# Attention rows of two units merged in DRAM, down weights loaded once a block, last block in two halves: a transformer pair of layers on one core

## The chip, the cores and the metric

One core of one Trainium2 chip. The metric is the device time of one execution in microseconds (us), taken over several executions; the profile is of one such execution, and its span is 2 to 3 us shorter than the time. Engines: PE (matmul; PEld is its weight loads), ACT (scalar engine: exponentials and GELU), DVE (vector engine), POOL, and SP, whose queue (SPq in the listings) issues nearly all the DMAs.

## The reference

Two layers with shared weights, S = 2048 tokens, D = 512, 32 heads of 16, F = 1792:

```python
x = x + A(layernorm(x), wqkv, wo)          # softmax attention, 32 heads of 16
x = x + B(layernorm(x), w_gate, w_up, w_down)  # (gelu(x@w_gate) * (x@w_up)) @ w_down
# ... the same two lines once more
```

## The kernel before

The kernel writes its program with a small list scheduler of its own: a model of each engine's time decides, while the program is built, in which fixed order the instructions stand. A "unit" is four heads of one block of 512 query rows; a layer has 4 blocks of 8 units, and a unit has 64 score tiles of 128 keys by 512 queries. Most tiles get their exponential on ACT, in instructions of two or three tiles. Some go to DVE, by an integer trick with one evacuation and three shifts ("vector tiles"). The feed-forward of a finished block ("post") is fed in pieces into the gaps of the next block's attention.

The parts that the change touches (cuts are marked `# ...`):

```python
NWR = 6                                   # slots for gate, up and down weight chunks, 256 KB each
OS = sb("fOS", [128, HB + 4, 512], F32)   # unnormalised attention rows, one slot a unit
RB = sb("fRB", [128, 2, 512], F32)        # broadcast reciprocals
ATS = sb("fATS", [128, 2, 512], F16)      # odd units' rows before they move to their partitions
# ...
for layer in range(n_rep):                # the list of weight loads, in order of use
    for qb in range(NQB):
        tail = layer == n_rep - 1 and qb == NQB - 1
        wlist += [("g", i) ...] + [("u", i) ...]
        wlist += [("d", i) for _ in range(1 if tail else 2 if qb == NQB - 1 and NQB > 1 else 4) for i in range(NFT // 2)]
# ...
def normalise(layer, qb, gs, half):       # for a group of units (four; 4, 2, 1, 1 at the very end)
    # ... check and reciprocal of the gathered denominators on DVE, stored to DRAM
    def spread():
        # per unit: four DMAs broadcast the reciprocals to RB, POOL multiplies OS by RB;
        # an even unit's product goes to AT, an odd unit's to ATS and by four DMAs to AT
        for j in range(4):
            move(0, "rb%d_%d" % (slot, j), RB[32 * j:32 * j + 16, slot, :], AP(RSC, ...), ...)
# ...
def post(layer, qb):
    # wait for the rows of all 8 units; output projection, layernorm,
    # 7 chunks of gate, GELU, 7 of up, then down for each token tile (weights loaded again)
# ...
def keep_clock():   # dummy matmuls, put in while PE would idle (meant to keep its clock up; no run here tests that)
    # four matmuls of 17x512, on zeros
```

A DMA is a job for SP: it is put into the queue in the order in which the model sees its inputs ready, and SP issues strictly in that order.

## Time and profile before

Median 1682.3 us (1681.39 to 1684.56, 3 runs).

| | before |
|---|---|
| span | 1680.1 us |
| end of the last attention product | 1610.4 us |
| tail after it | 69.7 us |
| ACT busy before that point / waits on scores | 1552.0 / 45.5 us |
| dummy matmuls, about 55 ns each | 2396 |

Lines of the page of the kernel before: busy time and share of each engine; ACT's busy tenths in 40 slices; the chain of waits by engine; and two groups of instructions (count, busy us, mean ns, then the idle time before them and its main cause).

```profile
PE 1574.3 (94%) x15555; PEld 490.9 (29%) x15614; DVE 1378.3 (82%) x2329; ACT 1561.3 (93%) x1348; POOL 208.6 (12%) x222
...
ACT  7899999999999999999899999999999999999932
...
ACT 53%; PE 34%; DVE 10%; POOL 1%; DMA 1%; issue 1%; SPq 0%; DVEq 0%; POOLq 0%
...
L1344 PE MATMUL fPS<-fONB,fZV 128*17 128x512 f16 x2396 | 186.5, 385 | 2.3 <-POOL fQMASK L362 1.5
...
L788 POOL TENSOR_TENSOR fAT<-fOS,fRB 128x512 f16<-128x512 f32 x32 | 43.1, 1345 | 815.6 <-DMA fRB<-rscr 815.6
```

PE's 94% is not work alone: the dummies (L1344) are in it, and their timeline (276 in 15.07 us) gives 131 us for all 2396. Apart from that, the Trainium skill ("Trainium Kernel Development and Optimization", section "Performance Expectations") calls matmul busy time a bad metric for the distance to the peak, because matmuls are pipelined. This trace agrees: a dummy's record is 385 ns long, and the dummies start 55 ns apart. POOL's 815.6 us of waiting costs nothing, as POOL is 12% busy and makes up 1% of the chain.

The waits of ACT (line, and what ended the wait: total us, times, longest):

```profile
ACT fPT L1204 <- PE fPS L1191: 45.5, 74, 5.3
ACT L919 <- PE fPS L592: 30.3, 1, 30.3
```

The windows view, cut at the end of the last attention product (each busy time in us, instructions in brackets):

```profile
core 0: us, PE busy (x) PEld busy (x) DVE busy (x) ACT busy (x) POOL busy (x), PEclk, DMA share, GB/s
0.00:1610.43 1610.43, 1510.60 (x14945) 461.85 (x15001) 1354.28 (x2282) 1551.98 (x1333) 205.85 (x218) 1.00 0.23 66
1610.43:1680.10 69.67, 63.73 (x611) 29.06 (x613) 24.03 (x47) 9.32 (x15) 2.78 (x4) 0.98 0.26 73
```

So ACT's time up to the last product is 1552.0 us busy and 58.4 idle, of which 45.5 are waits for scores.

The timeline of the tail of the kernel before (start us, length us, engine, line, operation, count; in brackets the idle time before it):

```profile
1610.47 0.69 DVE L829 COPY fOS<-fPS 128x512 f32<-128x512 f32 x1 [1.46 <-PE fPS L1324]
...
1611.21 15.07 PE L1344 MATMUL fPS<-fONB,fZV 128*17 128x512 f16 x276 [0.78 <-DVE fOS L829]
...
1615.99 1.69 SPq L277 DMA_DIRECT2D fRB<-rscr  x4
1619.20 1.28 POOL L788 TENSOR_TENSOR fATS<-fOS,fRB 128x512 f16<-128x512 f32 x1 [17.34 <-DMA fRB<-rscr]
1620.51 3.12 SPq L277 DMA_DIRECT2D fAT<-fATS  x4
...
1626.45 3.40 PE L592 MATMUL fPS<-fWO,fAT 128*128 128x512 bf16 x15 [0.16 <-issue]
...
1638.77 24.35 PE L592 MATMUL fPS<-fXNT,fWR 128*128 128x512 f16 x112
...
1663.17 12.03 PE L953 MATMUL fPS<-fWR,fHT 128*128 128x512 bf16 x54
...
1675.96 2.25 SPq L277 DMA_DIRECT2D out_dram<-fXNT  x4
```

Copy-out, normalisation behind four DMA hops while PE runs 276 dummies, projection at 1626.4, layernorm, 112 gate and up matmuls, down, stores. Elsewhere the two longest waits of ACT are 5.3 us near the start and this one at the layer boundary (timeline of the kernel before):

```profile
820.35 2.37 ACT L1204 ACTIVATE fPT<-fPS 128x1024 bf16<-128x1024 f32 x2 [4.79 <-PE fPS L1191]
```

### The profile page before, as it was taken

The numbers are of one execution on the slowest core, as the hardware profiler recorded it, in microseconds if no ns is written. First come the engines' busy times: TensorE is split into PE (matmuls) and PEld (weight loads), VectorE is DVE, ScalarE is ACT, GpSimd is POOL, SyncE is SP. The second block draws the span as 40 slices with busy tenths as digits, with TensorE's granted clock in tenths as the row PEclk, the third lists the DMA queues.
The fourth block names the chain that finished last, engine by engine and source line by source line (L and its number), as shares of the span: only waits on it lengthen the run. The fifth ranks groups of instructions, "written<-read, shape, count | busy, mean of one in ns | idle before, by whom it ended". The sixth has DMA issues, their size and how long they took to land.

```text
span 1680.1 us, 36981 instructions
## 1 busy us (share of the span) xinstructions
PE 1574.3 (94%) x15555; PEld 490.9 (29%) x15614; DVE 1378.3 (82%) x2329; ACT 1561.3 (93%) x1348; POOL 208.6 (12%) x222
## 2 busy tenths in 40 slices
PE   9999999999899989999999999999999999999998
PEld 3332222222222223233332322222222222222233
DVE  7899998879998799977643899988899878897853
ACT  7899999999999999999899999999999999999932
POOL 3222010101201021000600211101011100101010
PEclk9999999999999999999999999999999999999999
DMA  4100001252014410125224000024301251014303
GB/s 139 52 2 18 2 19 33 67 176 59 17 45 123 135 42 9 44 63 171 74 58 138 27 19 17 22 58 132 113 18 39 68 168 56 17 45 145 107 16 109
DMA packets 140285, 111.82 MB, mean 67 GB/s; under 512 B 13904, under 2 KB 129872, under 8 KB 140112
## 3 DMA queue, kind: packets, MB, share of 16 engines
q1 hardware_dynamic: 136416, 104.78, 21.5%
q0 software_dynamic: 2112, 4.19, 0.9%
q8 instruction: 127, 2.08, 0.5%
q10 hardware_dynamic: 1584, 0.39, 0.1%
q14 instruction: 46, 0.38, 0.1%
HBM read 97.78 MB, written 6.82 MB: 62 GB/s over the span
## 4 chain that ended last, share of the span: by engine, by line
ACT 53%; PE 34%; DVE 10%; POOL 1%; DMA 1%; issue 1%; SPq 0%; DVEq 0%; POOLq 0%
ACT fPT L1204 50%; PE fPS L592 10%; PE fPS L1324 9%; PE fPS L1191 8%; DVE fPP L1277 4%; PE fPS L953 3%; DVE fPI L1241 3%; PE fPS L1344 2%; ACT fHT L1157 2%; POOL fVD L669 1%; DVE fHT L916 1%; DVE fHT L939 1%; ACT L1157 1%; PE fPS L656 1%; DVE fQ L636 0%
## 5 line engine op out<-in xcount | busy, mean ns | idle before, releaser
L1204 ACT ACTIVATE fPT<-fPS 128x1536 bf16<-128x1536 f32 (+1 forms) x1302 | 1487.6, 1286 | 49.1 <-PE fPS L1191 45.5
L1241 DVE TENSOR_SCALAR fPI<-fPS 128x512 int16<-128x512 f32 x843 | 570.5, 684 | 94.0 <-PE fPS L1191 88.1
L1191 PE MATMUL fPS<-fQ,fKT 32*128 32x512 f16 x4096 | 513.6, 385 | 50.4 <-ACT fPT L1204 36.2
L1324 PE MATMUL fPS<-fPT,fVP 128*17 128x512 bf16 x3253 | 469.5, 383 | 11.7 <-DVE fOS L829 5.4
L1277 DVE TENSOR_SCALAR fPP<-fPI 128x2048 int16<-128x2048 int16 (+3 forms) x723 | 445.5, 646 | 8.1 <-PE fPS L1324 2.4
L1324 PE MATMUL fPS<-fPP,fVD 128*17 128x512 f16 x2529 | 410.0, 382 | 10.6 <-DVE fPP L1277 5.7
L1191 PEld LDWEIGHTS fPS<-fQ,fKT 32*128 32x128 f16 x4096 | 128.8, 91 | 535.3 <-ACT fPT L1204 383.8
L1324 PE MATMUL fPS<-fPI,fVP 128*17 128x512 f16 x843 | 255.1, 382 | 1.6 <-DVE fPP L1277 0.9
L592 PE MATMUL fPS<-fXNT,fWR 128*128 128x512 f16 x896 | 221.7, 381 | 10.9 <-DVE fHT L939 6.0
L1344 PE MATMUL fPS<-fONB,fZV 128*17 128x512 f16 x2396 | 186.5, 385 | 2.3 <-POOL fQMASK L362 1.5
L1324 PEld LDWEIGHTS fPS<-fPT,fVP 128*17 128x17 f16 x3253 | 108.8, 88 | 164.0 <-issue 92.6
L788 POOL TENSOR_TENSOR fAT<-fOS,fRB 128x512 f16<-128x512 f32 x32 | 43.1, 1345 | 815.6 <-DMA fRB<-rscr 815.6
L1324 PEld LDWEIGHTS fPS<-fPP,fVD 128*17 128x17 f16 x2529 | 99.3, 88 | 120.3 <-issue 47.4
L939 DVE TENSOR_TENSOR fHT<-fPS,fHT 128x512 bf16<-128x512 f32 x112 | 76.4, 688 | 57.6 <-PE fPS L592 41.2
L953 PE MATMUL fPS<-fWR,fHT 128*128 128x512 bf16 x402 | 113.7, 382 | 7.6 <-issue 5.7
L592 PEld LDWEIGHTS fPS<-fXNT,fWR 128*128 128x128 bf16 x896 | 72.8, 98 | 128.9 <-DVE fHT L939 19.6
L916 DVE CAST fHT<-fPS 128x512 bf16<-128x512 f32 x98 | 66.6, 686 | 25.7 <-PE fPS L592 25.3
L1344 PEld LDWEIGHTS fPS<-fONB,fZV 128*17 128x17 f16 x2396 | 56.3, 91 | 64.4 <-issue 30.6
L1324 PEld LDWEIGHTS fPS<-fPI,fVP 128*17 128x17 f16 x843 | 58.3, 88 | 37.5 <-issue 14.2
L669 POOL TENSOR_SCALAR fVD<-fVP 128x544 f16<-128x544 f16 (+1 forms) x48 | 54.7, 1142 | 96.4 <-DVE fVP L677 93.8
L548 POOL TENSOR_SCALAR fLNS<-fMV 128x4 f32<-128x4 f32 (+1 forms) x17 | 5.2, 306 | 430.5 <-DVE fMV L541 430.4
L788 POOL TENSOR_TENSOR fATS<-fOS,fRB 128x512 f16<-128x512 f32 x32 | 42.4, 1325 | 78.2 <-DMA fRB<-rscr 78.2
(60 smaller groups left out, 700.3 us busy)
## 6 DMA issues: line engine op xcount, KB each, us to landing
fWR<-in_B_w_down_dram SPq DMA_DIRECT2D x189, 256.0 KB, 3.0
fWR<-in_B_w_gate_dram SPq DMA_DIRECT2D x56, 256.0 KB, 3.1
fWR<-in_B_w_up_dram SPq DMA_DIRECT2D x56, 256.0 KB, 2.9
fRB<-rscr SPq DMA_DIRECT2D x256, 32.0 KB, 1.9
fX<-in_A_x_dram POOLq DMA_DIRECT2D x4, 1024.0 KB, 5.6
xscr<-fX SPq DMA_DIRECT2D x16, 256.0 KB, 2.5
fX<-xscr SPq DMA_DIRECT2D x4, 1024.0 KB, 5.6
fAT<-fATS SPq DMA_DIRECT2D x128, 16.0 KB, 1.8
```

Of the source, the lines that this page charges most:

```text
L592: ins = e.matmul(bank(bs[0])[:, 0:cols], lhsT=l, rhs=r_, start=(i == 0), stop=(i == n - 1))
L669: job("pool", 2, [(lambda e, dst=dst, src=src, ph=ph: e.tensor_scalar(dst, src, 2.0 ** (-ph / NPH), None, op0=ALU.mult), [("VP", c, k) for ...
L788: job("pool", 1, [(lambda e: e.tensor_tensor(dst, OS[:, os_, :], RB[:, slot, :], op=ALU.mult), [("OS", os_)] + [("RB", slot, j) for j in r ...
L916: evac_job(1, b, [(lambda e: e.tensor_copy(HT[:, ft, :], bank(b)), [BK[b]], [("HT", ft)], 0.6)], got(("gate", layer, qb, ft)))
L939: (lambda e: e.tensor_tensor(HT[:, ft, :], bank(b), HT[:, ft, :], op=ALU.mult), [BK[b], ("HT", ft)], [("HT", ft)], 0.62)], got(("up", laye ...
L953: ins = e.matmul(bank(b)[:, 0:D], lhsT=HT[:, ft, i * 128:(i + 1) * 128], rhs=WR[:, s, jj * D:(jj + 1) * D], start=(ft == 0), stop=(ft == N ...
L1191: ins = e.matmul(bank(b), lhsT=KT[32 * j:32 * j + 32, (u % NG) // 2, kt * 128:(kt + 1) * 128], rhs=Q[32 * j:32 * j + 32, (layer * NU + u) ...
L1204: o = sch.op("act", lambda e: e.activation(PT[:, p, 0:512 * na].rearrange("p (a b) -> p a b", a=na), PS[:, b0:b0 + na, :], ACTF.Exp, scale ...
L1241: dve(0, [(lambda e: e.tensor_scalar(PI[:, gi, 512 * r:512 * (r + 1)], bank(bd), DBIAS, 0.0, op0=ALU.add, op1=ALU.max), [BK[bd]], [("PI", ...
L1277: shifts.append((s, [(lambda e: e.tensor_scalar(PP[:, s, 0:512 * n], PI[:, gi, 0:512 * n], int(OCT) * ph // NPH, None, op0=ALU.add), [("PI ...
L1324: ins = e.matmul(PS[32 * j:32 * j + VW, ACC, :], lhsT=l, rhs=r_, start=a, stop=z, tile_position=(0, 32 * j), skip_group_check=True)
L1344: ins = e.matmul(PS[32 * j:32 * j + VW, ACC, :], lhsT=ZV[:, :], rhs=ones, start=False, stop=False, tile_position=(0, 32 * j), skip_group_c ...
```

## The change

The intent, as far as the code shows it: (1) rows of each unit are put out to DRAM at once; a pair of units then comes back as one full 128-partition tile, with one broadcast and one POOL product, so the odd rows need no second move. (2) That frees SBUF for a seventh weight slot, and down weights stay in seven slots for all token tiles of a block. (3) The last block's attention runs as two halves of 256 query rows, so that half of its feed-forward runs under the second half's attention; score tiles there are pairs of 256 columns. With them come smaller edits: keys and values of the second head group earlier at the start, pieces paced by cost with a tolerance for the first eight, and layernorm scales for two tiles at a time.

```diff
-    NWR = 6
+    NWR = 7
-    NOS = HB + 4
+    NOS = NPART + 1
-    NRB = 2
+    NRB = 1
-    ATS = sb("fATS", [128, 2, 512], F16)
+    OP = sb("fOP", [128, NRB, 512], F32)
+    OSD = nc.dram_tensor("oscr", (NOD // 2, 128, 512), F32, kind="Internal")
 # ... weight list: down once, the last block twice; six spare slots in WK, WV, WQ at the very end
+            halves = layer == n_rep - 1 and qb == NQB - 1 and NQB > 1
+            for h in ((0, 1) if halves else (None,)):
+                wlist += [("g", i) ...] + [("u", i) ...]
+                wlist += [("d", i) for i in range(NFT // 2)]
 # ... normalise: a pair comes back from DRAM, one product
+            move(0, "op%d" % slot, OP[:, slot, 0:qn], OSD[ds[0] // 2, :, 0:qn], ...)
+            move(0, "rb%d" % slot, RB[:, slot, 0:qn],
+                 AP(RSC, (half * NG + i) // 2 * 8 * 512, [[512, 8], [0, 16], [1, qn]]), ...)
+            # one POOL product into AT[:, c, q0:q0 + qn]
 # ... evac: each unit's rows go out by four DMAs; groups of 6 and 2 units
+            sizes = [NG - 2, 2] if NG > 2 else [NG]
+                    move(0, "os%d_%d" % (s, j), OSD[d // 2, 32 * j + 16 * (d % 2):..., 0:qn], OS[...], ...)
 # ... segments of the last block
+            for h in range(2):
+                segs += [(layer, NU - NG + g, HALF[h], 0, 2 * NKT) for g in order(layer, NQB - 1, h)]
 # ... start, pacing, layernorm
-                    kv(up, b, layer == 0)
+                    kv(up, b, layer == 0 and (up > 1 or b > PRE))
-                        pace["n"] += 1
+                        if first <= 8:
+                            p.tol = 1.0
+                        pace["n"] += (p.cost + 0.1) / 0.71
+        def scale(lo):      # layernorm scale and apply for two tiles
+            hi = min(lo + 2, nt)
 # ...
```

## The prediction

> **What bounds it now.** Busy table: PE 94%, ACT 93%, DVE 82%, POOL 12%; DMA 67 GB/s. Half of the chain of waits is the exponential on ACT. PE is not truly full: 2396 of its matmuls are clock-keeping dummies, about 55 ns each (276 in 15.07 us), some 131 us. ACT sets the pace until the last attention product at 1610.5 us; its score waits sum to 45.5 us, the longest near the start (5.3) and the layer boundary. Then a serial tail of 69.6 us, ACT nearly idle: copy-out and normalisation until 1626.4 (276 dummies), projection and layernorm until 1638.8, 112 gate/up matmuls 24.3, down 12.0, last adds and stores 4.9.
>
> **What changes.**
> 1. Merged rows: 64 POOL products (1.27 us) become 28 plus 8 half-wide, about 41 us for 85; 256 broadcast and 128 odd-row DMAs go, 288 put-outs, 36 loads and 36 broadcasts come. POOL is off the chain: about 0.
> 2. Down weights: 189 loads become 65, 32 MB less. The only weight landing on the chain was 4.9 us, with ACT still 98% busy. Worth 0 to 2 us.
> 3. Halves: half a feed-forward runs under the last attention. From the instruction order after the last attention product: 26 and 28 down of 512 columns and 8 projection (0.2165 us each), 112 gate/up of 256 columns (estimate 0.108, half of that), 444 dummies (0.0546). Sum 50 us, plus 0.5 copy-out and 4 at the end: a tail of 55 for 69.6. Gate/up saves 12, projection and layernorm 4, last adds 1. Down hardly shrinks: the first half's down spills past the attention. The wait before the projection stays: its broadcast is queued behind the first half's stores and weight loads, and 256 dummies precede it.
> 4. Cost: vector tiles 843 to 829, so 14 more on ACT (0.427 us by issue spacing) 6 us; two table loads 2.6; half a block's GELU 3.1: 12 us more ACT in the attention. PE: 14 us more real work.
> 5. Gains there: earlier keys and values at the start, gentler pacing, two-tile layernorms. Dummies before the tail fall from 1984 to 1692, 16 us of PE, most at the start and the layer boundary. I expect 10 to 16 of ACT's 45 us of score waits to go.
>
> **256 columns.** The Trainium skill, "TensorE: Matmul & The Clock Gate", gives a sustained spacing of about 81 ns at N=128, set by load and matmul together; this trace shows 16 matmuls of 128 columns in 1.07 us, about 57 ns apart. So no floor at 256; 0 to 5 us for the doubled issues.
>
> **Sum.** Attention ends near 1610 (+12, -13), then 55: time 1666 us. Range 1654 to 1679. Chances: faster by over 2% 0.10, within 2% 0.89, slower 0.01.
>
> **Right if:** the last attention product ends within 8 us of 1610.5; the tail is 52 to 58 us, with about 14 us of dummies directly before the projection and 12 us of gate/up; ACT is busy 12 us more before the tail; its score waits fall to 30 to 35 us; POOL falls to about 165 us; DMA falls by about 26 MB.
>
> **Wrong if:** PE falls behind in the last half block, where half a feed-forward meets attention at full rate in paired 256-column tiles (ACT's score waits rise near the end); the final broadcast, behind the weight loads in one issuing queue, lands after the dummies run out (tail 5 to 10 us longer); or more of the waits go, and the time nears 1655.

## The result, and the profile after

Median 1666.97 us (1666.56 to 1670.23, 4 runs) against 1682.48 (1681.39 to 1684.56, 4 runs). The ratio is 0.9911, 95% interval 0.9893 to 0.9928. Ratios here and below are the mean time of one kernel's runs over that of the other's of the same rounds, so not quite the ratio of the medians quoted.

The page of the changed kernel, the lines that answer to those above:

```profile
PE 1568.1 (94%) x16720; PEld 528.4 (32%) x16785; DVE 1361.7 (82%) x2335; ACT 1570.2 (94%) x1350; POOL 177.2 (11%) x230
...
ACT  6999999999999999999999999999999999999951
...
ACT 58%; PE 33%; DVE 6%; issue 1%; DMA 1%; POOL 1%; SPq 0%; DVEq 0%; POOLq 0%
...
L1507 PE MATMUL fPS<-fONB,fZV 128*17 128x512 f16 x2136 | 163.2, 385 | 1.7 <-POOL fQMASK L364 1.5
L878 POOL TENSOR_TENSOR fAT<-fOP,fRB 128x512 f16<-128x512 f32 (+1 forms) x36 | 43.3, 1204 | 979.7 <-DMA fRB<-rscr 979.7
```

Its waits of ACT:

```profile
ACT L1048 <- PE fPS L1026: 35.9, 1, 35.9
ACT fPT L1355 <- PE fPS L1341: 28.8, 65, 4.0
```

Its windows, cut at its last attention product (columns as before: PE, PEld, DVE, ACT, POOL):

```profile
0.00:1608.23 1608.23, 1517.08 (x16097) 500.29 (x16160) 1346.53 (x2305) 1565.06 (x1342) 175.31 (x226) 1.00 0.20 56
1608.23:1664.30 56.07, 51.04 (x624) 28.08 (x627) 15.21 (x30) 5.14 (x8) 1.88 (x4) 0.98 0.41 121
```

| us | before | after | change |
|---|---|---|---|
| ACT busy to the last product | 1552.0 | 1565.1 | +13.1 |
| ACT idle to the last product (waits on scores in it) | 58.4 (45.5) | 43.2 (28.8) | -15.3 (-16.7) |
| last product | 1610.4 | 1608.2 | -2.2 |
| tail | 69.7 | 56.1 | -13.6 |
| span | 1680.1 | 1664.3 | -15.8 |

The tail of the changed kernel on the timeline:

```profile
1608.28 0.42 DVE L913 COPY fOS<-fPS 128x256 f32<-128x256 f32 x1 [0.48 <-PE fPS L1487]
...
1608.96 0.59 SPq L279 DMA_DIRECT2D fLT<-fOS  x1
...
1613.14 0.59 DVE L846 SCALAR_TENSOR_TENSOR fOKL<-fLT,fOKL 16x128 f32<-16x128 f32 x2 [4.44 <-DMA fLT<-fOS]
1613.77 0.94 DVE L849 RECIPROCAL fLT<-fLT 16x128 f32<-16x128 f32 x1
...
1617.09 1.32 SPq L279 DMA_DIRECT2D rscr<-fLT  x2
1618.62 13.49 PEld L1507 LDWEIGHTS fPS<-fONB,fZV 128*17 128x17 f16 x256 [0.42 <-issue]
...
1619.18 2.62 SPq L279 DMA_DIRECT2D fWR<-in_B_w_up_dram  x5
1621.85 1.30 SPq L279 DMA_DIRECT2D out_dram<-fXNT  x2
1623.26 0.66 SPq L279 DMA_DIRECT2D fRB<-rscr  x1
1627.75 0.73 POOL L878 TENSOR_TENSOR fAT<-fOP,fRB 128x256 f16<-128x256 f32 x1 [19.96 <-DMA fRB<-rscr]
...
1632.77 1.67 PE L622 MATMUL fPS<-fWO,fAT 128*128 128x512 bf16 x7 [0.16 <-issue]
...
1641.19 1.64 PEld L1026 LDWEIGHTS fPS<-fXNT,fWK 128*128 128x128 bf16 x16
...
1660.39 1.70 SPq L279 DMA_DIRECT2D out_dram<-fXNT  x2
```

The PE lines are as predicted: 256 dummies directly before the projection take 14.0 us, 112 gate and up matmuls of 256 columns go from 1641.2 to 1653.6 (12.4 us). The SP lines show what happens meanwhile. The reciprocals are ready at 1614.7 but issued to DRAM at 1617.1. The broadcast, which needs only them (once they have landed), is issued at 1623.3, behind five weight loads and two stores. Its product is done at 1628.5. The dummies last till 1632.6, so for the last 4.3 us PE waits for no data that the profile shows: the order fixed beforehand had allowed for a later product.

Waits of ACT on scores by stretch, read from the waits view with a window, for every kernel that was run (us; "last" is the kernel's last attention product):

| kernel | 0-120 | 120-800 | 800-920 | 920-1400 | 1400-last | total | ACT busy to last | last product | tail | span |
|---|---|---|---|---|---|---|---|---|---|---|
| before | 10.7 | 14.9 | 7.6 | 8.3 | 4.0 | 45.5 | 1552.0 | 1610.4 | 69.7 | 1680.1 |
| after | 6.7 | 9.2 | 2.3 | 4.3 | 6.3 | 28.8 | 1565.1 | 1608.2 | 56.1 | 1664.3 |
| a_nohalves | 6.7 | 9.6 | 2.3 | 4.0 | 0.6 | 23.2 | 1553.0 | 1588.8 | 67.5 | 1656.3 |
| a_noearly | 10.7 | 6.3 | 3.1 | 5.4 | 6.7 | 32.1 | 1564.4 | 1612.0 | 54.0 | 1666.0 |
| a_oldpace | 6.6 | 5.3 | 2.9 | 5.0 | 6.9 | 26.7 | 1564.9 | 1606.0 | 53.5 | 1659.5 |
| a_jitter | 6.5 | 9.1 | 2.3 | 3.2 | 2.7 | 23.8 | 1563.6 | 1601.1 | 55.0 | 1656.1 |
| a_late | 6.7 | 9.1 | 2.3 | 3.4 | 6.3 | 27.7 | 1564.6 | 1606.9 | 45.6 | 1652.5 |
| b_merge | 10.5 | 9.6 | 9.6 | 8.9 | 2.0 | 40.7 | 1553.1 | 1608.2 | 66.2 | 1674.4 |
| a_reload | 6.5 | 7.8 | 2.4 | 7.1 | 4.8 | 28.7 | 1563.7 | 1606.2 | 64.2 | 1670.3 |
| a_ln4 | 6.5 | 7.9 | 2.5 | 5.4 | 4.1 | 26.4 | 1566.9 | 1608.8 | 53.6 | 1662.4 |
| b_both | 6.7 | 8.9 | 11.2 | 6.1 | 5.2 | 38.1 | 1554.5 | 1605.3 | 72.8 | 1678.1 |
| a_nh_old | 10.7 | 11.5 | 1.9 | 6.2 | 1.1 | 31.3 | 1557.7 | 1601.6 | 67.6 | 1669.2 |
| a_nh_jitter | 6.6 | 9.6 | 2.3 | 3.2 | 1.5 | 23.2 | 1554.3 | 1590.5 | 67.6 | 1658.1 |
| a_late_jitter | 6.7 | 9.2 | 2.3 | 2.1 | 2.8 | 23.0 | 1563.5 | 1600.5 | 46.9 | 1647.4 |

### The profile page after: what moved, and what is told of

The parts are those of the page before. It is cut to its first block, busy times and chain, and to the rows that moved or that the text cites. A ratio compares the mean times of both kernels' runs of the same rounds, so it can differ in the third digit from the quotient of the medians.

```text
span 1664.3 us, 39360 instructions
## 1 busy us (share of the span) xinstructions
PE 1568.1 (94%) x16720; PEld 528.4 (32%) x16785; DVE 1361.7 (82%) x2335; ACT 1570.2 (94%) x1350; POOL 177.2 (11%) x230
## 4 chain that ended last, share of the span: by engine, by line
ACT 58%; PE 33%; DVE 6%; issue 1%; DMA 1%; POOL 1%; SPq 0%; DVEq 0%; POOLq 0%
ACT fPT L1355 55%; PE fPS L1341 9%; PE fPS L1487 9%; PE fPS L1026 7%; PE fPS L1088 4%; ACT fHT L1304 3%; PE fPS L1507 2%; DVE fPI L1395 2%; PE fPS L622 2%; DVE fPP L1435 2%; DVE fHT L1045 1%; ACT L1304 1%; ACT L1355 1%; PE fPS L689 0%; SPq L279 0%
## 5 line engine op out<-in xcount | busy, mean ns | idle before, releaser
L1355 ACT ACTIVATE fPT<-fPS 128x1536 bf16<-128x1536 f32 (+1 forms) x1307 | 1494.9, 1281 | 32.7 <-PE fPS L1341 28.8
L1341 PE MATMUL fPS<-fQ,fKT 32*128 32x512 f16 (+1 forms) x4608 | 530.3, 359 | 55.6 <-ACT fPT L1355 36.7
L1487 PE MATMUL fPS<-fPT,fVP 128*17 128x512 bf16 (+1 forms) x3672 | 467.3, 359 | 6.4 <-DVE fOS L913 2.9
L1435 DVE TENSOR_SCALAR fPP<-fPI 128x2048 int16<-128x2048 int16 (+3 forms) x708 | 430.1, 639 | 7.4 <-PE fPS L1487 1.9
L1487 PE MATMUL fPS<-fPP,fVD 128*17 128x512 f16 (+1 forms) x2808 | 402.4, 357 | 5.9 <-DVE fPP L1435 2.6
L1487 PE MATMUL fPS<-fPI,fVP 128*17 128x512 f16 (+1 forms) x936 | 253.4, 357 | 1.5 <-DVE fPI L1395 0.5
L1026 PE MATMUL fPS<-fXNT,fWR 128*128 128x512 f16 (+1 forms) x952 | 220.0, 362 | 8.0 <-DVE fHT L1069 5.0
L1507 PE MATMUL fPS<-fONB,fZV 128*17 128x512 f16 x2136 | 163.2, 385 | 1.7 <-POOL fQMASK L364 1.5
L878 POOL TENSOR_TENSOR fAT<-fOP,fRB 128x512 f16<-128x512 f32 (+1 forms) x36 | 43.3, 1204 | 979.7 <-DMA fRB<-rscr 979.7
L1487 PEld LDWEIGHTS fPS<-fPP,fVD 128*17 128x17 f16 x2808 | 108.3, 89 | 111.8 <-issue 49.4
L1069 DVE TENSOR_TENSOR fHT<-fPS,fHT 128x512 bf16<-128x512 f32 x112 | 76.6, 689 | 46.5 <-PE fPS L1026 30.8
L913 DVE COPY fOS<-fPS 128x512 f32<-128x512 f32 (+1 forms) x72 | 45.1, 626 | 12.5 <-PE fPS L1487 12.0
L668 DVE TENSOR_SCALAR fQ<-fPS,fQMASK 128x512 f16<-128x512 f32 (+1 forms) x72 | 46.2, 684 | 7.6 <-PE fPS L622 7.6
```

Source lines behind the costliest of these rows:

```text
L1026: ins = e.matmul(bank(bs[0])[:, w * qn:(w + 1) * qn], lhsT=wchunk(s, (ft + w) % 2, ck), rhs=XNT[:, ck, xs], start=(ck == 0), stop=(ck == N ...
L1069: (lambda e: e.tensor_tensor(in_ht(ft), in_bank(b), in_ht(ft), op=ALU.mult), [BK[b]] + fk, fk, 0.62)], got(("up", layer, qb, h, ft))))
L1341: ins = e.matmul(bank(b)[:, b0:b0 + qn], lhsT=KT[32 * j:32 * j + 32, (x[1] % NG) // 2, kt * 128:(kt + 1) * 128], rhs=Q[32 * j:32 * j + 32, ...
L1355: o = sch.op("act", lambda e: e.activation(PT[:, p, 0:512 * na].rearrange("p (a b) -> p a b", a=na), PS[:, b0:b0 + na, :], ACTF.Exp, scale ...
L1435: shifts.append((s, [(lambda e: e.tensor_scalar(PP[:, s, 0:512 * n], PI[:, gi, 0:512 * n], int(OCT) * ph // NPH, None, op0=ALU.add), [("PI ...
L1487: ins = e.matmul(PS[32 * j:32 * j + VW, ACC, 0:qn], lhsT=l, rhs=r_, start=a, stop=z, tile_position=(0, 32 * j), skip_group_check=True)
```

## The experiments

Names starting with a_ are the changed kernel with an edit; b_ are the kernel before with a part of the change. All gave correct results. The runs of one batch share a chip and the runs of the kernel before: a_nohalves, a_noearly, a_oldpace and a_jitter; then a_late, b_merge, a_reload and a_ln4; then the last four.

### a_nohalves: the last block whole again

```diff
-            halves = layer == n_rep - 1 and qb == NQB - 1 and NQB > 1
+            halves = False
-    N_H = NU + NG if NQB > 1 else NU
+    N_H = NU
-    total_posts = n_rep * NQB + (1 if NQB > 1 else 0)
+    total_posts = n_rep * NQB
 # and the half segments and the two half cases of the pacing taken out
```

> The changed kernel with the last block whole again, everything else kept. My theory: the halves cut the tail but charge ACT for it, so they are worth little by themselves. From the order: 208 dummies before the projection and 140 after, 112 gate/up and 56 down of 512 columns, so a tail of about 65.5 us against 56.1; before the tail ACT loses half a block of GELU (3.1), two table loads (2.6) and 5 tiles (2.1), so the last attention product ends near 1600 instead of 1608.2. Span 1664 to 1670, ratio to before 0.990 to 0.995. Rival: the halves are the whole gain, the rest is worth 0: the tail's 13.4 us come back and the attention end stays, span 1676 to 1680, ratio 0.998 to 1.001.

Measured: 1657.66 us (before 1681.63), ratio 0.9854 (0.9837 to 0.987). This is faster than the changed kernel's 0.9911, beyond what either theory expected. Its windows, cut at its last attention product:

```profile
0.00:1588.78 1588.78, 1497.95 (x14695) 458.55 (x14750) 1333.07 (x2260) 1553.02 (x1336) 171.84 (x219) 1.00 0.19 55
1588.78:1656.30 67.52, 60.05 (x543) 27.30 (x545) 24.66 (x48) 9.32 (x15) 3.77 (x7) 0.97 0.17 51
```

Without the halves ACT is busy 12.0 us less before the last product (1565.1 against 1553.0), waits at the end are 5.7 us shorter (6.3 against 0.6), and the tail is 11.5 longer. So the rival falls: the halves are not the gain. Here they cost 8 us of span net. How much of that was luck of the order, the control tells. In this tail no weight load stands before the last broadcast: it is issued at 1595.6, 2.5 us after the store of the reciprocals, and the projection starts at 1601.2, 0.4 us after its product.

### a_jitter: a control that only reorders

```diff
-    WAIT_D = 0.45
+    WAIT_D = 0.47
```

> A control: the changed kernel with one constant of the scheduler moved from 0.45 to 0.47 us, which changes the order of instructions but no part of the change. It shows how far the time moves from reordering alone. I expect ratio 0.989 to 0.993, within 3 us of the changed kernel; a larger step would mean that differences of a few us between the other variants cannot be put down to their edits. The rival has nothing to say here.

Measured: 1659.53 us, ratio 0.9873 (0.9857 to 0.9889): 8 us of span less than the changed kernel, where I expected 3 at most. Its windows:

```profile
0.00:1601.07 1601.07, 1513.29 (x16116) 496.34 (x16178) 1342.17 (x2295) 1563.57 (x1343) 179.13 (x226) 1.00 0.20 56
1601.07:1656.10 55.03, 48.20 (x559) 27.14 (x561) 15.99 (x32) 5.14 (x8) 1.88 (x4) 0.99 0.47 132
```

A constant that means nothing moves the last product by 7 us: waits are 5.0 us lower in total, most of it after 1400 us (2.7 against 6.3), and ACT is busy 1.5 us less. So differences of a few us in time between two variants do not show the effect of an edit. The account by stretch is steadier: the waits before 920 us are the same to 0.2 us.

### a_nh_jitter: the second pair with and without halves

The edits of a_nohalves and a_jitter together.

> The run without halves, with the scheduler constant of the control at 0.47: a second pair with and without halves, to see whether the first pair was luck of the order. If the halves cost what the first pair showed (12 us more ACT, tail 11.5 shorter, waits at the end 4 to 6 longer), ACT before the last product is near 1552 here against 1563.6 in the control, the tail is 67.5 against 55.0, and the time is within 4 us of the control (about equal, the halves worth nothing): ratio 0.985 to 0.989. If halves truly pay, this is 6 us or more slower than the control, ratio above 0.991.

Measured: 1659.22 us (before 1681.97), ratio 0.986 (0.9845 to 0.9875). The control with halves has 0.9873, so time is equal within the intervals. ACT is busy 9.3 us less (1554.3 against 1563.6), the tail is 12.6 longer (67.6 against 55.0), and waits after 1400 us are 1.2 shorter. Both pairs agree in kind: the halves buy a tail 11.5 to 12.6 us shorter with 9.3 to 12.0 us of ACT. Of this ACT time 8.0 us are named by the profile: two GELU instructions of 1792 columns (3.3), two table loads (2.6), and five fewer vector tiles in each pair (an estimate of 2.1: five times the 0.42 us by which an ACT instruction of three tiles, 1498 ns in the kernel before, is longer than one of two, 1075 ns). The rest, 1 to 4 us, I have not located.

### a_noearly: without the earlier keys and values

```diff
-                    kv(up, b, layer == 0 and (up > 1 or b > PRE))
+                    kv(up, b, layer == 0)
-   ... (layer or up < 2 or started_all()) ...
+   ... (layer or not up or started_all()) ...
```

> The changed kernel without the early keys, values and queries of the second head group at the start. My theory: this part is worth 3 to 5 us of ACT's waits near the start (score waits before 120 us go back from 6.7 to about 10.7 us, ACT busy there from 104.9 to about 101), given back in part by a tail whose order is 2 us shorter: ratio 0.990 to 0.995. Rival: the gain of the attention part comes from the merged rows and the lighter DMA, so this is worth nothing: ratio 0.990 to 0.992 with the early waits unchanged at 6 to 7 us.

Measured: 1667.7 us, ratio 0.9914 (0.99 to 0.9928). Waits before 120 us are 10.7 us again, the very number of the kernel before, so the early start is worth 4.0 us there. The time hardly shows it, since the waits between 120 and 800 us happened to be 2.9 lower and the tail 2.0 shorter.

### a_oldpace: the pacing of before

```diff
-                        if first <= 8:
-                            p.tol = 1.0
-                        pace["n"] += (p.cost + 0.1) / 0.71
+                        pace["n"] += 1
-    PIECES = (4 * (4 * MM + 0.1) + ...) / 0.71
+    PIECES = 4 + 8 + 4 * NFT
```

> The changed kernel with feed-forward pieces counted as before (one each) and the first eight without their tolerance. My theory: pacing is worth some 4 us of score waits between 120 and 1400 us (from 15.8 back towards 30.8), ratio 0.991 to 0.995. Rival (merged rows and lighter DMA made these waits fall): waits stay near 16 us, ratio 0.990 to 0.992.

Measured: 1660.53 us, ratio 0.9874 (0.9858 to 0.9889). Waits between 120 and 1400 us came to 13.2 us, below the changed kernel's 15.8. My theory that pacing took them away falls, in the presence of the other parts. The ratio is also below the rival's range, by the size of the control's effect.

### b_merge: the merged rows alone

The allocations, `normalise`, `spread` and `evac` of the changed kernel put into the kernel before; six weight slots, down weights loaded again, whole blocks.

```diff
 # the kernel before, with
+    OP = sb("fOP", [128, NRB, 512], F32)
+    OSD = nc.dram_tensor("oscr", (NOD // 2, 128, 512), F32, kind="Internal")
+            sizes = [NG - 2, 2] if NG > 2 else [NG]
 # and the normalise of the changed kernel
```

> The kernel before with the merged rows alone (put out to DRAM, one broadcast and one product a pair, groups of six and two). My prediction said about 0 in the attention: score waits within 5 us of 45.5, POOL 30 to 40 us lower, and only the order's 68 fewer dummies before the last projection (3.7 us) to gain: ratio 0.996 to 0.999. Rival, raised by the run that undid the pacing and did not bring the waits back: the merge is what made them fall; then waits between 120 and 1400 us fall from 30.8 to about 16 and the ratio is 0.986 to 0.991.

Measured: 1673.98 us (before 1682.71), ratio 0.9945 (0.9926 to 0.9965). The tail is 3.5 us shorter (66.2), as the order told. POOL is busy 167.3 us against 208.6, and DMA moves 126.5 MB against 111.8. Waits are 40.7, which is 4.8 lower: within the 5 us that I had allowed, and far from the rival's 15. The ratio is a little under the 0.996 that I had stated, with an interval that reaches it.

### a_reload: down weights for every token tile again

```diff
-                wlist += [("d", i) for i in range(NFT // 2)]
+                n_d = 1 if tail else 2 if h is not None or qb == NQB - 1 and NQB > 1 else 4
+                wlist += [("d", i) for _ in range(n_d) for i in range(NFT // 2)]
-                if ts is groups[-1]:
-                    wdone(wds[k])
+                wdone(wds[k])
```

> The changed kernel with the down weights loaded again for every token tile, in its seven slots. My prediction: worth 0 to 2 us, so waits between 120 and 1400 us stay at 12 to 20 us and the time within the 8 us that the control showed for reordering: ratio 0.987 to 0.993. Rival: the lighter DMA took the waits away; they rise to about 30 us there and the ratio to 0.995 to 1.0.

Measured: 1670.54 us, ratio 0.9923 (0.9904 to 0.9943). DMA moves 134.0 MB instead of 97.3, and waits between 120 and 1400 us are 17.3 us, so the lighter DMA is not what took them away. But the tail is 64.2 us instead of 56.1. In the order, 384 dummies stand before the projection in place of 256, and the down matmuls of the first half stand in pairs with 4 to 24 dummies between them (1607.5 to 1617.7), about the time that their second loads go out. I take these gaps for the order's allowance for those loads, which is argued and not shown; the profile records only one wait on a DMA there, of 0.4 us, as the order is fixed beforehand. The projection starts at 1638.5, 5.8 us after the product that it needs. Five other kernels of the same tail lie between 53.5 and 56.1, so this is no reordering. Loading down once is worth some 8 us here, in the tail and only there.

### a_ln4: layernorm of four tiles in one go

```diff
-        def scale(lo):
-            hi = min(lo + 2, nt)
-            # ...
+        ln_scale(len(tts), got(("lns", name)))
+        if check:
+            ln_check(len(tts))
```

> The changed kernel with the layernorm of four tiles in one go again. Theory now: the two-tile layernorm is a candidate for the waits that fell at the layer boundary (800 to 920 us: 7.6 before, 2.3 after). If so they return to about 7 there, and the ratio is 0.990 to 0.996. If not, they stay at 2 to 3 and the time stays within the control's 8 us, 0.986 to 0.992.

Measured: 1664.26 us, ratio 0.9891 (0.9873 to 0.991). The wait at the boundary stays at 2.5 us, so the two-tile layernorm is not its cause. POOL is busy 166.9 us instead of 177.2: the two-tile version costs POOL 10 us, which is why my figure of 165 failed.

### b_both and a_nh_old: a square of pacing against memory

b_both is the kernel before with the early start and the new pacing. a_nh_old is the changed kernel without halves and with the edits of a_noearly and a_oldpace undone as above, so merged rows, down weights once, seven slots and the two-tile layernorm are left.

```diff
 # b_both: the kernel before, with
-                    kv(up, b, layer == 0)
+                    kv(up, b, layer == 0 and (up > 1 or b > 1))
-                        pace["n"] += 1
+                        if first <= 8:
+                            p.tol = 1.0
+                        pace["n"] += (p.cost + 0.1) / 0.71
 # a_nh_old: a_nohalves with the edits of a_noearly and a_oldpace
```

> The kernel before with only the early start and the new pacing (piece costs, tolerances): one corner of a square whose other corners are the kernel before, the run without halves (early start, pacing, merged rows, down weights once, two-tile layernorm) and the next run (the last three alone). Theory A: early start and pacing took the waits away: score waits fall to 6 to 7 us before 120 us and to about 16 between 120 and 1400 us (from 30.8), the last attention product comes near 1593, ratio 0.988 to 0.991 with the old tail of 69.7. Theory B: the merged rows and the down weights took those between 120 and 1400: they stay near 30, only the first 4 us go, ratio 0.996 to 0.999.

> The changed kernel without halves, without the early start and with the old pacing: what is left is merged rows, down weights once, seven slots and the two-tile layernorm. Theory A: waits 120 to 1400 us stay near 30, those before 120 near 10.7; only the tail's 2 us and little else gained, ratio 0.996 to 0.999. Theory B: waits 120 to 1400 fall to about 16, the last product near 1593, tail 67.5, ratio 0.987 to 0.991. If both this run and the last stay above 24, it takes both.

Measured: b_both 1680.32 us, ratio 0.9993 (0.9979 to 1.0007); a_nh_old 1670.58 us, ratio 0.9928 (0.9915 to 0.9942), beside 1681.97 before. The waits on scores in the square:

| total waits (us) | old start and pacing | new start and pacing |
|---|---|---|
| old rows, down reloaded | 45.5 (before) | 38.1 (b_both) |
| merged rows, down once, seven slots, two-tile layernorm | 31.3 (a_nh_old) | 23.2 (a_nohalves) |

The waits add up almost exactly: start and pacing take 7.4 or 8.1 us, the memory group takes 14.2 or 14.9. Each corner is a single profile, and the control moved the total by 5.0. The memory group's share is clear of that. Of the other, 4.0 us fall before 120 us in both rows and are the early start's; the remaining 3.4 or 4.1 do not show that pacing took anything. For the layer boundary the memory group alone decides: 7.6 and 11.2 us without it, 1.9 and 2.3 with it. Neither theory was right about the stretch from 120 to 1400 us as a whole: 26.2 us of waits in b_both, 19.6 in a_nh_old, 30.8 before, 15.9 with both. The time does not add up like this. b_both gains nothing in time, since its tail came out 3.1 us longer (in part because its projection waited 1.4 us for the odd rows' DMA, after its dummies; in the kernel before it followed them within 0.2) and ACT was busy 2.5 us more. On this much a single profile cannot say what is the edit and what is the order.

### a_late: the tail's weight loads behind the last broadcast

```diff
     def wfeed():
         while wst["loaded"] < len(wlist):
             i = wst["loaded"]
+            if i >= w_tail + 2 and NQB > 1 and not rel[0]:
+                break
 # ... in spread, when both loads of the pair are issued
+                if len(here) == 2 and (layer, qb, h) == (n_rep - 1, NQB - 1, 1) and gs[i + 1] == NG - 1:
+                    rel[0] = True
+                    wfeed()
```

> The changed kernel with all but the first two weight loads of the last half block issued only after the last broadcast of the denominators; the order of PE before the last attention product is unchanged (1692 dummies), after it 124 dummies stand before the projection in place of 336. My theory: the wait before the projection is made by the issuing queue, where that broadcast stood behind weight loads and stores (issued at 1623.3, its product done at 1628.5, the projection at 1632.8). Expected: projection about 12 us after the last attention product's copy-out instead of 24, tail about 44.5 us for 56.1, ratio 0.983 to 0.986. Rival: the wait is the chain of four DMA hops itself; then the projection still waits for the data about 20 us after the copy-out, and the later weight loads stall the gate matmuls too: tail 52 us or more, ratio 0.988 to 0.992.

Measured: 1657.33 us (before 1682.71), ratio 0.9852 (0.9835 to 0.9869). The attention part is the same instruction for instruction on PE, and ends at 1606.9; the tail is 45.6 us. Its timeline:

```profile
1609.22 0.59 DVE L850 SCALAR_TENSOR_TENSOR fOKL<-fLT,fOKL 16x128 f32<-16x128 f32 x2 [1.81 <-DMA fLT<-fOS]
1609.85 0.94 DVE L853 RECIPROCAL fLT<-fLT 16x128 f32<-16x128 f32 x1
...
1610.82 1.32 SPq L279 DMA_DIRECT2D rscr<-fLT  x2
...
1615.39 4.50 PE L1514 MATMUL fPS<-fONB,fZV 128*17 128x512 f16 x80
...
1616.95 0.66 SPq L279 DMA_DIRECT2D fRB<-rscr  x1
...
1619.25 4.75 SPq L279 DMA_DIRECT2D fWR<-in_B_w_up_dram  x6
1619.99 0.72 POOL L885 TENSOR_TENSOR fAT<-fOP,fRB 128x256 f16<-128x256 f32 x1 [15.23 <-DMA fRB<-rscr]
1620.77 1.41 PEld L626 LDWEIGHTS fPS<-fWO,fAT 128*128 128x128 f16 x8 [1.39 <-POOL fAT L885]
```

The reciprocals end at 1610.79 and are issued at 1610.82, where the changed kernel held them for 2.4 us. The built order now has 80 dummies before the projection in place of 256, and the projection starts at 1620.8 where it started at 1632.8. A wait is left: the broadcast is issued at 1616.95, behind two stores of the first half that wait for DVE's last add (it ends at 1616.2). The feed-forward did not pay for its later loads: the six up loads go out from 1619.25 on, and gate and up run from 1629.4 to 1641.8 without a gap. So the rival falls: the chain of DMA hops does not need 20 us, and the loads issued ahead of it made it longer. But they did so in more ways than my theory had it. From copy-out to projection the two kernels differ by 10.7 us (24.5 against 13.8), and the two timelines split it up: 2.4 is the store of the reciprocals held in the queue; 2.6 is their being ready earlier, mostly as the gathered denominators took 1.8 us from issue to use in place of 4.2; 1.5 is a shorter way from the broadcast's issue to its product (3.0 against 4.5); and 4.2 is the dummies, which no longer outlast the product. The time from the store of the reciprocals to the broadcast's issue, on which my theory rested, is 6.1 us in both. What slowed the gather and the broadcast, with many loads in flight at that time, was not tried apart.

The Trainium skill ("DMA: Bandwidth & Descriptors", section "Anatomy of one DMA — SWDGE (gpsimd) path") says that DMA engines do not wait on semaphores and that any such wait happens on the issuing sequencer before dispatch. That section is on DMAs issued by POOL; SP's queue in this trace agrees: two stores that waited for DVE took 3.65 us of the queue (1613.19 to 1616.84), and the broadcast behind them came 0.1 us later.

### a_late_jitter: the candidate

The edits of a_late and a_jitter together.

> The candidate for a better version: the changed kernel with the tail's weight loads behind the last broadcast, in the order of the control (0.47). From the order of PE: 92 dummies before the projection instead of 260 in the control, 12 more among the gate matmuls, so a tail about 8 us shorter than the control's 55.0; the attention part is the control's, last product near 1601. Expected span 1647 to 1650, ratio 0.981 to 0.984. Against: weights land too late and gate matmuls stall, tail 50 or more, ratio 0.985 or above.

Measured: 1649.35 us (1648.82 to 1650.24, 5 runs; before 1681.97), ratio 0.9805 (0.9791 to 0.9818). Its windows:

```profile
0.00:1600.50 1600.50, 1521.90 (x16177) 495.90 (x16178) 1340.57 (x2295) 1563.53 (x1343) 178.39 (x226) 1.00 0.20 56
1600.50:1647.40 46.90, 40.47 (x405) 22.91 (x405) 15.99 (x32) 5.25 (x8) 1.89 (x4) 0.98 0.54 154
```

This beats both kernels. The interval straddles 2%, so whether it is faster by more than that is open. It is 17.6 us under the changed kernel's median, a comparison of different rounds (the ratios to the kernel before are 0.9805 and 0.9911); by the profiles about half comes from the later loads (the tail is 46.9 instead of the control's 55.0) and half from the control's luckier order (1656.1 against 1664.3). With the loads moved the halves pay in this order: it is 10.7 us of span under a_nh_jitter, where the plain control was only 2.0 under it. In the other order they do not: a_late's 0.9852 and a_nohalves' 0.9854 are equal. So whether the halves pay is open.

## Why the prediction was right

The time, 1666.97 us, is 1 us from the predicted 1666, and the sum was right in its large terms too. Point by point:

- **ACT sets the pace until the last product; the halves charge ACT 12 us.** Right in total: 13.1 us more before the last product, 9.3 and 12.0 in the two pairs with and without halves. The term of tiles was put in the wrong place: of the 14 tiles that moved to ACT only five go with the halves.
- **Tail of 55 us for 69.6.** Right: 56.1. The dummies before the projection took 14.0 us (about 14), gate and up 12.4 (12), and a_late shows that the loads ahead of the broadcast lengthen the wait, as I had said: moving them took 10.5 us off the tail. The reason given, the broadcast's place in the queue, is only part of it: 2.4 us are a store held in the queue, about 4 are DMAs whose data came sooner, and 4.2 are dummies that outlasted the product.
- **Attention still ends near 1610.** Right: 1608.2. Waits fell to 28.8, a little under the 30 to 35 forecast. The control, a mere reordering, ended its attention at 1601.1, outside the 8 us that I had set as a test.
- **Where the waits went.** Wrong in the cause. I gave them all to the early start, gentler pacing and the two-tile layernorm, and about 0 to merged rows and down weights in the attention. The square shows 7.4 to 8.1 us for start and pacing, of which only the start's 4.0 are clear of the scatter, and 14.2 to 14.9 for the memory group. Within this group merged rows alone took 4.8, no more than the scatter; undoing the reload or the two-tile layernorm alone brought nothing back. What carries the rest, the seventh slot, the feeding of slots as they come free, or two of these together, was not tried and stays open.
- **Down weights worth 0 to 2 us.** Wrong in size with the halves: a_reload's tail is 8 us longer. Nothing in the attention, as said.
- **DMA falls by 26 MB.** Wrong: 14.6 MB (111.8 to 97.3). The halved block loads its weights twice (97.3 against 91.6 MB without halves), and the merge adds 14.7 MB (b_merge), not the 6 I had worked out.
- **POOL at 165 us.** Wrong: 177.2; the products came to 43.3 us where about 41 was forecast, and the two-tile layernorm adds 10.
- **256 columns cost 0 to 5 us.** The tail shows no floor: 110 ns for each of 112 matmuls. After 1400 us waits rose from 4.0 to 6.3 us, but in the control they fell to 2.7. Beside the same kernels without halves (0.6 and 1.5) they are 5.7 and 1.2 us higher: a little past the range in the first pair, within it in the second. What part of this is the doubled issues was not tried.

The closeness of the number owes something to chance: a meaningless constant moves this kernel by 8 us of span, and the range of 1654 to 1679 was about right for that.

## What to carry to other kernels

Account a change as busy time, idle time and tail of the engine that paces, and measure what mere reordering does before crediting an edit with a few microseconds; waits by stretch separate causes that the total time mixes. Work pulled out of a serial tail is not free when it lands on the pacing engine: here a tail 12 us shorter was paid with 9 to 12 us of ACT, and even with the weight loads moved behind the tail's critical DMAs it paid off in one of two orders. In a program of fixed order, look also at whether the work put in to fill a wait outlasts the wait: here it did by 4.3 us.

## What the Trainium skill lacked or had wrong

- "TensorE: Matmul & The Clock Gate", section "Back-to-back issue gap", gives sustained spacings of about 81 ns at N=128 and 131 at N=512 for streams of load and matmul, and calls its formula N/2.4 + 2.5 an isolated figure. Here such streams, each matmul with its own weights, ran at about 57 ns (16 of 128 columns in 1.07 us, the last of them 0.22 long), 110 ns (112 of 256 columns in 12.34 us) and 217 ns (112 of 512 columns in 24.3 us): the formula, not the sustained figures.
- "DMA: Bandwidth & Descriptors" says that semaphore waits happen at issue, but not what an in-order issuing queue costs a later, urgent DMA: the store of the ready reciprocals was issued 2.4 us late behind weight loads, and at once when these came later; with that, with data that came sooner from other DMAs and with fewer dummies, the tail fell from 56.1 to 45.6 us.
- No page has the scatter of a statically ordered program: a change of order alone moved the span from 1664.3 to 1656.1 us.
